# A recurrent attention and two experts on one core: weights to floats in fewer VectorE steps, and TensorE tied to the written order

## The chip, the cores and the metric

The kernel runs on one core of a Trainium2 chip. The metric is the time of one execution on the device in microseconds (us), the median of several runs. The kernel before takes 1247.12 us (three runs, 1245.66 to 1247.34). A core has TensorE (PE in the profile; its weight loads are PEld), VectorE (DVE), ScalarE (ACT), GpSimd (POOL) and SyncE (SP, which issues most of the DMAs here).

## What is computed

Three stages follow each other. The sizes are batch 4, 8 heads, 768 steps of time, head size 40; 3072 tokens of width 320; 2048 and 1536 columns in the two experts.

```
# 1. attention: a 40x40 state per batch and head, updated at each of 768 steps
y[t]  = r[t] @ state
Sa    = state @ a[t]
state = state * w[t] - outer(Sa, b[t]) + outer(v[t], k[t])
# 2. first expert
h = x @ w_in;  g = max(h, 0) + alpha * min(h, 0);  x = g @ w_out
# 3. second expert
g = x @ w_gate;  out = (silu(g) * (x @ w_val)) @ w_out
```

The weights of the experts arrive as 64-bit floats, since the reference multiplies by a 64-bit scalar when it draws them. The kernel reads them as pairs of 32-bit words and makes 32-bit floats of them itself.

## The kernel before, in words

**Blocks and items.** Time is cut into six blocks of 128 steps (m = 0 to 5), each with four items, one for each batch row. An item holds all eight heads and is worked in two chunks of 64 steps (`L`).

**Preparing an item** (`prep_a`, `prep_b`, seven steps). Scans on VectorE make running products of the decays w (L502, L509), a product of these with a gives the tile `AN` (L519, two halves of 64 partitions; the other halves are zeroed by GpSimd, L517), one with b and k gives `kbt` (L531). Then TensorE forms 16 products `mnp` (L543) and 8 transposes `kbp` (L571), which ScalarE and GpSimd bring to SBUF. The raw inputs w and a lie in one tile `raw_wa`, loaded by two DMAs an item.

**The inverse** (`inverse`, forty steps, once a block). When four items are prepared, their 64 by 64 triangular matrices are inverted: 31 small steps on VectorE, each a product and a subtraction (L604, L612), between transposes (L589 ahead, L615 and L617 behind), and then small matmuls on TensorE (L625, L644). Its work tiles share their buffers (tag "kbt") with `kbt` of the preparation from block one on, so that the next block's preparation starts behind the inverse.

**Running an item** (`seq`, thirteen steps). The state goes from chunk to chunk: a chunk transposes the state into `sp` (L707, copied to `s0` by ScalarE, L709), and then forms `zp` (L714), `pp` (L724, with transposes L730), `gp` (L741) and `yp` (L756, L760), one after the other in one PSUM buffer of its chain, with copies by ScalarE and VectorE between. Two chains of items run side by side. The result goes to DRAM (`xd`).

**The first expert on a block** (`mlp1`). For each of 16 slices of 128 columns ("groups" below): eight matmuls of 512 columns up (L238), ReLU on ScalarE (L277), the leaky part on VectorE (L278), a split into a high and a low part (L184, L185), and eight matmuls down (L243 to L249). A block is 36 steps: a load of x, two steps a group, and three that bring out the result.

**Weights.** `conv` loads 128 rows or columns of a weight, `narrow` makes floats, `split` cuts them, and they go back to DRAM (`wd`), from where `fetch` takes them for each block. `narrow` is three VectorE steps on the two words (L172 to L174), an absolute value on ScalarE (L175), and a comparison that sets tiny values to zero: on VectorE (L177) for the 32 pieces of the first expert, on GpSimd (L179, L180) for others. The first expert's pieces are converted beside blocks zero and one (`conv1`), those of the second partly beside the last blocks (`conv2`, 12 pieces), partly in the tail (`direct`, 24 pieces).

**What sets the order.** The program is written by `drive`, which takes steps from several generators in turn, so that each is about equally far along; each generator's weight is its number of steps. A planner then places the instructions of every engine by priority (`tc.cur_priority`, lower is earlier) and by simulated times. Preparing, inverting and running items have priorities 3000 ahead (`SQ`, `PRI`), so that matmuls of the first expert fill in behind. In turn m of the main loop stand together: running block m, preparing and inverting block m+1, and the first expert on block m-1, all 36 steps of it; in the last turn 15 of them are held back for the tail, where the first expert on block five follows.

**The second expert** runs at the end alone, six blocks of 12 slices.

Of the kernel before, what the change touches and what calls it, by code (L numbers as in the profile page):

```python
# [9 lines left out]
U32 = mybir.dt.uint32  # L10
ACTF = mybir.ActivationFunctionType
# [4 lines left out]
FAC = 1.0  # L16
# [48 lines left out]
LOOK = 2  # L65
KEEP = 4

@with_exitstack
def kernel(
# [50 lines left out]
    def drive(*gens, lead=0, engs=0, lag=1, who=0):  # L120
        live = [[*g, 0, j] for j, g in enumerate(gens)]
        names = ["PE", "DVE", "Activation", "Pool"]
        while live:
            e = min(live, key=lambda e: e[3] / e[1])
            try:
                tc.cur_priority -= e[2]
                with ExitStack() as st:
# [6 lines left out]
                    ok = next(e[0], 0)  # L134
                    if e[4] < lead:
# [6 lines left out]
                e[3] += 1  # L142
# [21 lines left out]
    LEAST = 1.125 * 2.0 ** -15  # L164

    def narrow(pool, raw, dve=0):
        whi, wlo = raw[..., 1], raw[..., 0]
# [19 lines left out]
    def conv(stage, idx, src, f, kind, into=None, dve=None):  # L187
# [10 lines left out]
        w32 = narrow(stage, raw, idx < 2 * K1 if dve is None else dve)  # L198
# [196 lines left out]
    for j, pool in ((0, rawp), (1, bp)):  # L395
        for nm in ("wa", "bk"):
            t = raw[nm, j] = pool.tile([128, 2, NP, TB], F32, name=f"raw_{nm}{j}")
            for n in range(2):
                for q in (1, 3):
                    eng = nc.vector if nm == "wa" and j == 0 else nc.gpsimd  # L400
                    eng.memset(t[32 * q:32 * q + 32, n], 1.0 if (nm, n) == ("wa", 0) else 0.0)
# [43 lines left out]
    def load(i, nm):  # L445
# [3 lines left out]
        t = raw[nm, rset(i)]  # L449
        for h, pr in enumerate(halves):  # L450
            nc.sync.dma_start(out=t[pr], in_={"wa": wa, "bk": bk}[nm][m, bb, h])
# [40 lines left out]
    def prep_a(i):  # L492
        m, bb = order[i]
        it = items[i] = {}
        rw = raw["wa", rset(i)][:, 0]
# [18 lines left out]
        ra = raw["wa", rset(i)][:, 1]  # L514
# [71 lines left out]
    def inverse(m):  # L586
# [8 lines left out]
        for kk in range(HALF - 1):  # L595
# [17 lines left out]
            yield  # L613
# [41 lines left out]
    N_PREP, N_INV, N_SEQ, N_MLP = 7, 40, 13, 2 * K1 + 4  # L655
# [5 lines left out]
    def seq(i, ch, own=None):  # L661
# [33 lines left out]
        for c in range(CPB):  # L695
# [9 lines left out]
            sp = ps_s.tile([128, NP // 2, 128], F32, tag=sb, name="sp")  # L705
            for q in range(NP // 2):
                nc.tensor.transpose(sp[:, q, :], st[:, 2 * q:2 * q + 2, :].rearrange("q p d -> q (p d)"), ident)  # L707
            s0 = seq_p.tile([128, NP // 2, 128], F32, tag="s0", name="s0")
            nc.scalar.copy(out=s0, in_=sp)  # L709
            yield  # L710
# [16 lines left out]
            for h in range(2):  # L727
                nc.scalar.mul(out=pv[:, h::2, c, h], in_=pp[:, 0, h::2], mul=-1.0)
# [302 lines left out]
```

## Time and profile before

| | |
|---|---|
| median of three runs | 1247.12 us |
| span of the profiled execution | 1243.4 us |
| PE busy, PEld busy | 1095.8 us (88%), 928.7 us (75%) |
| DVE, ACT, POOL busy | 781.3, 592.6, 312.6 us |
| the chain that ended last, by engine | PE 52%, DVE 20%, ACT 10%, DMA 8%, issue 6% |

The span is the time from the first to the last instruction of the execution that was profiled; its own time is the span and what lies around it, and the runs' median is 3.7 us above the span. A row of the window view gives the busy time of each engine in a stretch, in brackets its instructions, then TensorE's granted clock (1.00 is 2.4 GHz, 0.50 is 1.2 GHz), the DMA engines' share and GB/s. A row of the line view gives busy time and the mean ns of one instruction, and behind the second bar the idle time of the engine just ahead of them with what ended it.

### The profile page before, as it was taken

Reading aid. Unit: us, or ns where it says so; the run is one execution under the profiler, and the core shown is the slowest. Engines: PE = TensorE matmul, PEld = TensorE weight load, DVE = VectorE, ACT = ScalarE, POOL = GpSimd, SP = SyncE. Lnnn points to the kernel's source line nnn. Section 1 sums busy time; section 2 is a strip of 40 time slices with the busy share of each in tenths; the row PEclk is TensorE's granted clock in tenths of the full one; section 3 lists DMA queues with packets and bytes.
Section 4 is the critical chain, followed back from the end, with each engine's and each line's share of the span. In section 5 each row is a group of like instructions: output and inputs, shape, how many; then the busy total and the mean of one; then the engine's idle time right before and its main releaser. Section 6 shows DMA issues by size and latency. Waiting matters only on the chain.

```text
span 1243.4 us, 24467 instructions
## 1 busy us (share of the span) xinstructions
PE 1095.8 (88%) x9056; PEld 928.7 (75%) x9056; DVE 781.3 (63%) x1689; ACT 592.6 (48%) x1463; POOL 312.6 (25%) x502
## 2 busy tenths in 40 slices
PE   3345787899799989989999899999999999999998
PEld 2244577777687777777777687888888888888887
DVE  7999999898669758974967444677732323232222
ACT  4547448844763674477455533455432323232222
POOL 9425443613121222252126300334500000000000
PEclk9658697999899999999999999999999999999999
DMA  5534577874545454464448648865210101000000
GB/s 149 168 115 133 180 257 251 263 228 126 161 127 176 134 161 142 144 196 145 145 139 266 201 131 292 283 213 153 73 47 1 47 1 38 1 22 1 22 1 22
DMA packets 92486, 166.36 MB, mean 134 GB/s; under 512 B 12752, under 2 KB 42704, under 8 KB 92368
## 3 DMA queue, kind: packets, MB, share of 16 engines
q1 hardware_dynamic: 84208, 160.87, 41.2%
q10 hardware_dynamic: 8160, 3.93, 1.1%
q8 instruction: 72, 1.18, 0.4%
q14 instruction: 46, 0.38, 0.1%
HBM read 136.98 MB, written 27.79 MB: 133 GB/s over the span
## 4 chain that ended last, share of the span: by engine, by line
PE 52%; DVE 20%; ACT 10%; DMA 8%; issue 6%; POOL 3%; SPq 1%; ACTq 0%; DVEq 0%; POOLq 0%
PE pg L238 10%; PE pv L238 10%; PE u L238 8%; PE o L952 3%; PE o L951 3%; PE o L953 3%; DVE la L612 3%; DVE tmp L604 3%; DMA raw_wa<-in_wa_dram 2%; PE gp L741 2%; PE d L243 2%; DMA xa<-xd 2%; PE d L244 2%; PE d L245 2%; DVE gs L685 2%
## 5 line engine op out<-in xcount | busy, mean ns | idle before, releaser
L184 ACT CAST gh<-g 128x512 fp32r<-128x512 f32 (+1 forms) x176 | 105.9, 602 | 175.2 <-DVE g L967 116.7
L967 DVE TENSOR_TENSOR g<-pv,sg 128x512 f32<-128x512 f32 x72 | 49.8, 691 | 200.1 <-PE pv L238 200.0
L185 DVE TENSOR_TENSOR gl<-g,gh 128x512 fp32r<-128x512 f32 (+1 forms) x176 | 119.5, 679 | 77.0 <-ACT gh L184 76.2
L238 PE MATMUL u<-xh,wt 128*128 128x512 f32 (+1 forms) x416 | 147.6, 397 | 15.9 <-DVE g L278 12.6
L278 DVE SCALAR_TENSOR_TENSOR g<-g,neg,u 128x512 f32<-128x512 f32 (+1 forms) x104 | 72.9, 701 | 63.0 <-ACT g L277 62.4
L238 PEld LDWEIGHTS u<-xh,wt 128*128 128x128 f32 x416 | 79.0, 193 | 34.9 <-DVE g L278 16.8
L238 PE MATMUL pg<-xh,w 128*128 128x512 f32 x288 | 102.0, 394 | 0.7 <-ACT sg L965 0.7
L965 ACT ACTIVATE sg<-pg 128x512 f32<-128x512 f32 x72 | 43.0, 597 | 124.3 <-PE pg L238 124.3
L238 PE MATMUL pv<-xh,w 128*128 128x512 f32 x288 | 100.5, 389 | 0.0
L277 ACT ACTIVATE g<-u 128x512 f32<-128x512 f32 (+1 forms) x104 | 58.7, 564 | 81.6 <-PE u L238 65.0
L543 PE MATMUL mnp<-AN,kbt 128*128 128x128 f32 x384 | 60.7, 311 | 32.1 <-POOL la L591 15.9
L952 PE MATMUL o<-w,gh 128*128 128x320 f32 x288 | 87.7, 309 | 0.0
L951 PE MATMUL o<-w,gh 128*128 128x320 f32 x288 | 87.1, 308 | 0.0
L244 PE MATMUL d<-gl,wt 128*128 128x512 f32 (+1 forms) x208 | 80.9, 391 | 1.2 <-DVE gl L185 1.2
L699 POOL COPY gs<-raw_v 64x160 f32<-64x160 f32 x96 | 42.3, 441 | 157.7 <-PE yp L756 70.1
L543 PEld LDWEIGHTS mnp<-AN,kbt 128*128 128x128 f32 x384 | 54.3, 219 | 36.2 <-POOL AN L517 17.6
L604 DVE TENSOR_TENSOR tmp<-la 128x96 f32<-128x96 f32 (+43 forms) x306 | 78.6, 281 | 3.2 <-POOL la L592 1.3
L238 PE MATMUL u<-xl,wt 128*128 128x512 f32 (+1 forms) x208 | 80.2, 386 | 0.2 <-DVE xl L185 0.2
L612 DVE TENSOR_TENSOR la<-la,tmp 128x96 f32<-128x96 f32 (+43 forms) x306 | 77.6, 278 | 1.9
L245 PE MATMUL d<-gh,wt 128*128 128x512 f32 (+1 forms) x208 | 78.5, 380 | 0.0
L557 POOL TENSOR_SCALAR_AFFINE_SELECT AN<-AN 64x256 f32<-64x256 f32 x96 | 48.5, 505 | 117.9 <-ACT AN L556 88.8
L953 PE MATMUL o<-w,gl 128*128 128x320 f32 x288 | 76.1, 309 | 0.0
(118 smaller groups left out, 2678.6 us busy)
## 6 DMA issues: line engine op xcount, KB each, us to landing
wt<-wd SPq DMA_DIRECT2D x98, 384.0 KB
wt<-wd SPq DMA_DIRECT2D x98, 320.0 KB
wd<-wc SPq DMA_DIRECT2D x24, 384.0 KB
raw<-in_moe_w_out_dram SPq DMA_DIRECT2D x28, 320.0 KB
raw_wa<-in_wa_dram SPq DMA_DIRECT2D x48, 160.0 KB
raw_bk<-in_bk_dram SPq DMA_DIRECT2D x48, 160.0 KB
wd<-wc SPq DMA_DIRECT2D x20, 320.0 KB
raw<-in_moe_w_in_dram SPq DMA_DIRECT2D x16, 256.0 KB
```

The lines of the kernel that those rows point to most:

```text
L184: nc.scalar.copy(out=h, in_=raw)
L185: eng.tensor_tensor(out=l, in0=raw, in1=h.bitcast(F32), op=ALU.subtract)
L238: nc.tensor.matmul(ps, lt, rh, start=(i == 0), stop=(i == len(ops) - 1))
L244: nc.tensor.matmul(ps, wh, gl, start=False, stop=False)
L245: nc.tensor.matmul(ps, wl, gh, start=False, stop=last)
L278: nc.vector.scalar_tensor_tensor(g, g, neg[:, f:f + 1], ps, ALU.mult, ALU.add)
L543: nc.tensor.matmul(ps[:, s].rearrange("p h t -> p (h t)"), kbt[:, g * SH + s].rearrange("p j t -> p (j t)"), an[:, :, g * SH + s, :],)
L604: nc.vector.tensor_tensor(out=tv, in0=ml[:, kk + 1:HALF, kk:kk + 1].to_broadcast([128, nr, ns]), in1=tl[:, kk:kk + 1, c0:c0 + ns].to_broad ...
L612: mark["inv"] = nc.vector.tensor_tensor(out=dst, in0=dst, in1=tv, op=ALU.subtract)
L951: nc.tensor.matmul(ops[q], gh[:, ts], wh, start=first, stop=False)
L952: nc.tensor.matmul(ops[q], gh[:, ts], wl, start=False, stop=False)
L953: nc.tensor.matmul(ops[q], gl[:, ts], wh, start=False, stop=last)
```

## The change

Weights: `narrow` lets ScalarE scale the high word by 2^-112 and make a float's three last bits of the low word's upper 16 bits, and then takes two VectorE steps; the comparison is gone, on either engine. Preparation: w and a get tiles of their own; a lies in a tile whose cross halves are zero from the start, and `AN` is one VectorE instruction over 128 partitions and 1024 elements. An item's w and a are loaded by four DMAs of half the size. Running: the transposes of the state move behind `pp`, into its PSUM buffer, and their copy behind that of the U part; the stage of its own for `sp` goes. Order: from turn two on (`TIE`), each TensorE instruction depends on the one written ahead of it, and the priorities there are zero; the second chain starts half a step later; a step of the inverse counts 0.6 of a step; the first expert runs 6 of its steps later (`LAG`), which is three slices of two steps, and 19 steps are left for the tail, 4 more than before.

```diff
-        nc.vector.tensor_scalar(y, whi, 0x07FFFFFF, 3, ALU.bitwise_and, ALU.logical_shift_left)
-        nc.vector.scalar_tensor_tensor(z, whi, 0xC0000000, y, ALU.bitwise_and, ALU.bitwise_or)
-        nc.vector.scalar_tensor_tensor(y, wlo, 29, z, ALU.logical_shift_right, ALU.bitwise_or)
-        nc.scalar.activation(out=f, in_=whi.bitcast(F32), func=ACTF.Abs)
-        if dve:
-            nc.vector.scalar_tensor_tensor(f, f, LEAST, y.bitcast(F32), ALU.is_ge, ALU.mult)
-            return f
-        nc.gpsimd.tensor_scalar(f, f, LEAST, None, ALU.is_ge)
-        nc.gpsimd.tensor_tensor(out=f, in0=f, in1=y.bitcast(F32), op=ALU.mult)
+        nc.scalar.activation(out=f, in_=whi.bitcast(F32), func=ACTF.Copy, scale=2.0 ** -112)
+        nc.scalar.activation(out=y, in_=wlo, func=ACTF.Copy, scale=2.0 ** -13, bias=2.0 ** -14 - 0.5)
+        nc.vector.scalar_tensor_tensor(y, whi, 0x80000000, y, ALU.bitwise_and, ALU.bitwise_or)
+        nc.vector.scalar_tensor_tensor(z, z, 3, y, ALU.logical_shift_left, ALU.bitwise_or)
...
+    def tied(new):
+        for x in new:
+            if x.engine == nc.tensor.engine:
+                if tail_pe:
+                    tc.add_manual_dep(
+                        x, tail_pe.pop().name,
+                        mybir.DependencyInfo(mybir.DependencyClass.NoSync, mybir.DependencyReason.DATA),
+                        reason="order of TensorE",
+                    )
+                tail_pe.append(x)
...
-            nc.sync.dma_start(out=t[pr], in_={"wa": wa, "bk": bk}[nm][m, bb, h])
+            if nm == "wa":
+                nc.sync.dma_start(out=raw["w", rset(i)][pr, 0], in_=wa[m, bb, h][:, 0])
+                nc.sync.dma_start(out=raw["a", rset(i)][pr, h], in_=wa[m, bb, h][:, 1])
...
-        for h, pr in ((0, hi), (1, lo)):
-            nc.gpsimd.memset(an[pr, h], 0.0)
-        for h, pr in ((0, lo), (1, hi)):
-            (nc.gpsimd if i >= B and ANP >> h & 1 else nc.vector).tensor_tensor(
-                out=an[pr, h], in0=ra[pr].rearrange(seg, c=CPB), in1=wx[pr, ::-1, 0:L], op=ALU.mult
-            )
+        nc.vector.tensor_tensor(
+            out=an, in0=raw["a", rset(i)].rearrange("q h p (c t) -> q h (p c) t", c=CPB),
+            in1=wx[:, ::-1, 0:L].unsqueeze(1).to_broadcast([128, 2, NSEG, L]), op=ALU.mult,
+        )
...
-    N_PREP, N_INV, N_SEQ, N_MLP = 7, 40, 13, 2 * K1 + 4
+    N_PREP, N_INV, N_SEQ, N_MLP = 7, 9 + (HALF - 1) * INVW, 13, 2 * K1 + 4
...
-            sp = ps_s.tile([128, NP // 2, 128], F32, tag=sb, name="sp")
...
+            sp = pp[:, 0].rearrange("p (a b) t -> p a (b t)", b=2)
...
+    gm = chain(*gms)
+    held = 2 * (K1 - HOLD) + 3 + HELD
     for m in range(1, NM):
         s0_ = m * B
+        sp_, hp_ = (0, 0) if m >= TIE else (SQ, HP)
...
-        gm = gms[m - 1]
-        nm = N_MLP + (1 if FA and m == 1 else 0)
-        held = 2 * (K1 - HOLD) + 3 if m + 1 == NM else 0
-        g.append((take(gm, nm - held), nm, 0))
...
-        drive(*g, lead=2, engs=G2, lag=LG2, who=W2)
...
+        nm = N_MLP - (LAG if m == 1 else held - LAG if m + 1 == NM else 0)
+        g.append((take(gm, nm), nm, 0))
+        drive(*g, tie=m >= TIE)
```

## Rows read from the trace of the kernel before

**Rows 1.** The windows view: stretches between ends of inverses, and what follows.
```profile
78.00:190.00 112.00, 81.30 (x994) 70.57 (x996) 106.29 (x267) 67.01 (x196) 48.84 (x76) 0.78 0.57 182
190.00:300.00 110.00, 97.36 (x1070) 84.67 (x1067) 99.05 (x239) 71.11 (x204) 39.54 (x65) 0.91 0.72 227
...
411.00:522.00 111.00, 101.16 (x1113) 83.07 (x1112) 83.00 (x207) 65.77 (x178) 25.43 (x53) 1.00 0.51 151
...
632.00:750.00 118.00, 109.12 (x1138) 87.69 (x1137) 64.98 (x113) 58.64 (x144) 41.12 (x53) 0.99 0.59 185
750.00:854.00 104.00, 101.67 (x432) 81.56 (x430) 66.51 (x106) 50.32 (x90) 29.17 (x27) 0.98 0.73 247
```

**Rows 2.** The chain of waits around 300 us (start, us, what).
```profile
299.56 2.00 DVE tt L617
```

**Rows 3.** The windows view of line L172 alone: pieces of weights converted.
```profile
78.00:190.00 112.00, 6.81 (x17) 0.78 0.57 182
190.00:300.00 110.00, 4.12 (x9) 0.91 0.72 227
```

**Rows 4.** The chain of waits in the tail: matmuls of 512 columns.
```profile
1227.11 1.81 PE pv L238 x8
```

**Rows 5.** The timeline of PE: runs of one kind (start, us, what).
```profile
411.88 1.15 PE L724 MATMUL pp<-tt,zs 128*64 128x64 f32 x32
412.96 2.21 PE L625 MATMUL eps<-la,tt 32*32 32x32 f32 x128
415.11 0.50 PE L243 MATMUL d<-gh,wt 128*128 128x512 f32 x1
...
564.52 1.95 PE L741 MATMUL gp<-rbd,pv 128*128 128x128 f32 x16
566.30 0.27 PE L571 MATMUL kbp<-ident,kbt 128*128 128x128 f32 x1
...
569.72 0.93 PE L756 MATMUL yp<-gs,KB 128*64 128x104 f32 x16
570.49 0.61 PE L760 MATMUL yp<-rbd,s 128*64 128x128 f32 x8
570.92 0.88 PE L756 MATMUL yp<-gs,KB 128*64 128x104 f32 x16
```

**Rows 6.** The windows view of line L278 alone: groups of the first expert.
```profile
411.00:522.00 111.00, 9.64 (x13) 1.00 0.51 151
...
632.00:750.00 118.00, 12.63 (x17) 0.99 0.59 185
750.00:854.00 104.00, 18.62 (x25) 0.98 0.73 247
```

**Rows 7.** The line view: the inverse's steps, `narrow`, `AN` and `kbt`.
```profile
L604 DVE TENSOR_TENSOR tmp<-la 128x96 f32<-128x96 f32 (+43 forms) x306 | 78.6, 281 | 3.2 <-POOL la L592 1.3
...
L612 DVE TENSOR_TENSOR la<-la,tmp 128x96 f32<-128x96 f32 (+43 forms) x306 | 77.6, 278 | 1.9
...
L173 DVE SCALAR_TENSOR_TENSOR wz<-raw,wy 128x384 uint32<-128x384 uint32 (+1 forms) x68 | 47.6, 700 | 3.6 <-POOL w L185 1.7
...
L174 DVE SCALAR_TENSOR_TENSOR wy<-raw,wz 128x384 uint32<-128x384 uint32 (+1 forms) x68 | 45.0, 661 | 0.9
...
L175 ACT ACTIVATE wz<-raw 128x384 f32<-128x384 f32 (+1 forms) x68 | 36.1, 531 | 63.4 <-DVE wy L174 37.7 <-issue 8.8 <-POOL la L592 4.1
...
L519 DVE TENSOR_TENSOR AN<-raw_wa,Wx 64x512 f32<-64x512 f32 x48 | 35.4, 737 | 1.1
...
L531 DVE TENSOR_TENSOR kbt<-raw_bk,rest 128x1024 f32<-128x1024 f32 x24 | 30.5, 1269 | 7.8 <-PE kbp L571 6.8 <-PE eps L625 0.8
...
L172 DVE TENSOR_SCALAR wy<-raw 128x384 uint32<-128x384 uint32 (+1 forms) x68 | 27.1, 399 | 21.7 <-POOL wz L180 17.1 <-DMA raw<-in_moe_w_val_dram 2.2 <-DMA raw<-in_moe_w_out_dram 1.1
...
L177 DVE SCALAR_TENSOR_TENSOR wz<-wz,wy 128x384 f32<-128x384 f32 (+1 forms) x44 | 23.8, 542 | 10.1 <-ACT wz L175 9.8
```

**Rows 8.** The view of waits: us in total, times, longest us.
```profile
PEld zp L714 <- ACT s L709: 18.8, 13, 5.0
```

More of the change, by code (lines that the diff above doesn't have):

```diff
@@ L10 @@
 U32 = mybir.dt.uint32
+U16 = mybir.dt.uint16
 ACTF = mybir.ActivationFunctionType
@@ L65 @@
 LOOK = 2
+LAG = 6
+HELD = 4
+INVW = 0.6
+TIE = 2
 KEEP = 4
@@ L118, in traced, with drive @@
         return nc.cur_bb.bb.instructions
-    def drive(*gens, lead=0, engs=0, lag=1, who=0):
-        live = [[*g, 0, j] for j, g in enumerate(gens)]
+    tail_pe = []
+    def tied(new):
[8 more added lines that the diff above has]
+                tail_pe.append(x)
+    def drive(*gens, lead=0, engs=0, lag=1, who=0, tie=False):
+        live = [[*g[:3], g[3] if len(g) > 3 else 0, j] for j, g in enumerate(gens)]
         names = ["PE", "DVE", "Activation", "Pool"]
@@ L134, in drive @@
                     ok = next(e[0], 0)
+                    if tie:
+                        tied(traced()[n0:])
                     if e[4] < lead:
@@ L185, in split, with conv @@
         eng.tensor_tensor(out=l, in0=raw, in1=h.bitcast(F32), op=ALU.subtract)
-    def conv(stage, idx, src, f, kind, into=None, dve=None):
+    def conv(stage, idx, src, f, kind, into=None):
         sw = words(src)
@@ L395 @@
     for j, pool in ((0, rawp), (1, bp)):
-        for nm in ("wa", "bk"):
-            t = raw[nm, j] = pool.tile([128, 2, NP, TB], F32, name=f"raw_{nm}{j}")
-            for n in range(2):
+        for nm in ("w", "bk"):
+            sh = [128, 2, NP, TB] if nm == "bk" else [128, 1, NP, TB]
+            t = raw[nm, j] = pool.tile(sh, F32, name=f"raw_{nm}{j}")
+            for n in range(sh[1]):
                 for q in (1, 3):
-                    eng = nc.vector if nm == "wa" and j == 0 else nc.gpsimd
-                    eng.memset(t[32 * q:32 * q + 32, n], 1.0 if (nm, n) == ("wa", 0) else 0.0)
+                    eng = nc.vector if nm == "w" and j == 0 else nc.gpsimd
+                    eng.memset(t[32 * q:32 * q + 32, n], 1.0 if nm == "w" else 0.0)
+        t = raw["a", j] = pool.tile([128, 2, NP, TB], F32, name=f"raw_a{j}")
+        (nc.vector if j == 0 else nc.gpsimd).memset(t, 0.0)
         if j == 0:
@@ L732, in seq @@
                 )
+            for q in range(NP // 2):
+                nc.tensor.transpose(sp[:, q, :], st[:, 2 * q:2 * q + 2, :].rearrange("q p d -> q (p d)"), ident)
             for h, pr in ((0, lo), (1, hi)):
@@ L737, in seq @@
                 )
+            s0 = seq_p.tile([128, NP // 2, 128], F32, tag="s0", name="s0")
+            nc.scalar.copy(out=s0, in_=sp)
             yield
@@ L870 @@
         )
+    gm = chain(*gms)
+    held = 2 * (K1 - HOLD) + 3 + HELD
     for m in range(1, NM):
         s0_ = m * B
+        sp_, hp_ = (0, 0) if m >= TIE else (SQ, HP)
         g = [
-            (chain(seq(s0_, 0), seq(s0_ + 2, 0)), 2 * N_SEQ, SQ),
-            (chain(seq(s0_ + 1, 1), seq(s0_ + 3, 1)), 2 * N_SEQ, SQ),
+            (chain(seq(s0_, 0), seq(s0_ + 2, 0)), 2 * N_SEQ, sp_),
+            (chain(seq(s0_ + 1, 1), seq(s0_ + 3, 1)), 2 * N_SEQ, sp_, .5),
         ]
         if m + 1 < NM:
-            g.append((chain(preps(range((m + 1) * B, (m + 2) * B)), lift(inverse(m + 1), PV)), FAC * (B * N_PREP + N_INV), HP))
-        gm = gms[m - 1]
-        nm = N_MLP + (1 if FA and m == 1 else 0)
-        held = 2 * (K1 - HOLD) + 3 if m + 1 == NM else 0
-        g.append((take(gm, nm - held), nm, 0))
-        if not CG:
-            g.append((take(c2, CS[m - 1]), CS[m - 1], 0))
-        drive(*g, lead=2, engs=G2, lag=LG2, who=W2)
-        if CG:
-            for _ in take(after(mark["inv"], c2), CS[m - 1]):
-                pass
-        assert held or next(gm, 0) == 0
+            g.append((chain(preps(range((m + 1) * B, (m + 2) * B)), lift(inverse(m + 1), PV)), FAC * (B * N_PREP + N_INV), hp_))
+        nm = N_MLP - (LAG if m == 1 else held - LAG if m + 1 == NM else 0)
+        g.append((take(gm, nm), nm, 0))
+        drive(*g, tie=m >= TIE)
+        for _ in take(after(mark["inv"], c2), CS[m - 1]):
+            pass
     ap_.close()
```

32 lines of the change are left out of this document (14 added, 18 removed).

## The prediction

> **What bounds the kernel now.** I read the windows first [rows 1], cut where an inverse ends (L617; the one at 299.56 us stands in [rows 2]), then the lines, then runs of matmuls in the timeline. They show three regimes. Up to 300 us VectorE is the full engine: 106.29 of 112 us and 99.05 of 110 us, while TensorE has 81.30 and 97.36 at a granted clock of 0.78 and 0.91, between its two levels of 1.2 and 2.4 GHz [rows 1]. In this stretch the first expert's 32 pieces of weights are made floats; 17 and 9 of them fall into these two windows, the other 6 ahead [rows 3]. From 300 to 750 us neither engine is full by itself: in 411 to 522 us VectorE has 83.00 of 111 us, ScalarE 65.77, TensorE 101.16 by its spans [rows 1]. These spans overlap and include stalls, so I count TensorE's work at the pace of clean runs. From 750 us on one stream of matmuls follows another and little is to be won.
>
> The paces: 512 columns take 1.81/8 = 0.227 us [rows 4]; 128 columns on the full array (566.30 - 564.52)/16 = 0.111; `yp` 0.77/16 = 0.048 and its second part 0.43/8 = 0.054; `pp` 1.08/32 = 0.034; the inverse's small ones 2.15/128 = 0.017 [rows 5]. A group of the first expert is 16 matmuls of 512 columns, 3.63 us. Attention of one block, counts from the code: 64 `mnp`, 32 `kbp`, 64 `gp`, 32 transposes of state and U at 0.111 make 21.3 us; 128 `yp` 6.2, 64 of its second part 3.5, 128 `pp` 4.3, 128 `zp` at the pace of `pp` 4.3, 256 of the inverse 4.3: 43.9 us. The window 411 to 522 us holds 13 groups [rows 6], 47.2 us; with 43.9 that is 91.1 of 111 us, a share of 0.82. The last, 632 to 750 us, holds 17 groups (61.7 us) and attention without preparation and inverse (96 matmuls and 256 fewer: 43.9 - 10.7 - 4.3 = 28.9 us), 90.6 of 118 us, 0.77. Three blocks of 91.1 and this one make 364 of 450 us: 0.81.
>
> The Trainium skill ("Perfetto Trace Analysis", section "Identifying the Most-Contended Engine") says that the busy time of matmuls misjudges TensorE's headroom, and that the busy share of weight loads is the measure. By matmul spans 10 us of the 111 would be idle, by weight loads (83.07) 28 us; the count above gives 20, between them. By the matmul spans, about 10 us in each of four blocks would be all that an order could win.
>
> **The change part by part.**
>
> *Floats, first expert.* A piece loses four VectorE steps, 0.399 + 0.700 + 0.661 + 0.542 = 2.30 us, and gets two of the two-operand kind. No row shows their exact operations; the nearest are L173 and L174, mean 0.68, so 1.36 us, and 0.94 us are saved [rows 7]. Between 78 and 300 us that is 26 x 0.94 = 24.4 us. The 6 pieces ahead stand beside loads and the first inverse; I count 2 us of their 5.6. ScalarE gets one activation more, about 0.53 us [rows 7], 13.8 us in a stretch where it has 138 of 222 us [rows 1]: its room covers it. If it had none, those 13.8 us would come off the gain. If VectorE runs these steps only where it would else be idle, the gain is nothing; if the two new steps ran at the 0.54 of L177, it would be 1.22 x 32 = 39 us.
>
> *AN.* Twice 0.737 becomes one instruction of the shape of `kbt`, 1.269 us [rows 7]: 0.2 us saved an item, 1.6 us for the 8 items of blocks one and two, in the same full engine. Two GpSimd memsets an item go too; GpSimd is at 49 of 112 us, so I cost this at nothing. Four loads for two: 48 DMA issues more on SP in all. The w tile is free after its copy already, the a tile only after `AN`; an a load that waits holds the second w load and whatever is behind in SP's queue, as the combined load did. I cost it at nothing, and between -3 and +3 us.
>
> Together the stretch to 300 us shortens by 24.4 + 2 + 1.6 = 28 us, to 272, bounds 0 to 40. What is late next there is the inverse's own chain, and TensorE, whose clock can only gain from denser work.
>
> *Order, lag and held steps.* These say what each turn must hold. Turn one gets 30 of the first expert's steps, turns two to four 36 each, which is 16 groups, and turn five 36 - (19 - 6) = 23, of which 6 finish block three's expert (1.5 groups and three steps of result), one loads x and 16 are 8 groups: 9.5 groups. So TensorE's work is 3 x (58.0 + 43.9) = 305.7 us and 34.5 + 28.9 = 63.4 us, together 369 us between 272 us and the end of attention. Before, 13 groups fitted in a turn and the backlog was worked off in the last; with the order tied, a turn cannot end ahead of its 16 groups.
>
> At what share will TensorE run? Not below the present 0.81 if the waits are the same ones; not above 1. What speaks for more: `zp` no longer stands behind the copy of the state, for which the weight loads alone waited 18.8 us [rows 8]; expert matmuls come in whole steps between those of attention, where before they filled in behind; and x is loaded 6 steps into a turn, not right behind its store. The nearest row for a stream whose order is that of the program, with the same activations on ScalarE and VectorE between, is 750 to 854 us: 25 groups, 90.7 of 104 us, 0.87 [rows 1, 6]. I take 0.87: 369/0.87 = 424 us, where 0.81 gives 455 and 1 gives 369. A turn is then 101.9/0.87 = 117 us, longer than today's 111, and the last 73 where it was 118.
>
> *Moved transposes.* Their count stays (32 a block with those of U). They now wait for the two negated copies of `pp`, and `gp`, written after them, is held in TensorE's queue; `gp` needs these copies anyway. In the share above; alone between -5 and +2 us a block.
>
> *Second expert's floats.* 12 pieces beside the last blocks and 24 in the tail lose a VectorE step or two and two of GpSimd. TensorE is at 101.67 of 104 us there [rows 1]; nothing.
>
> *The tail.* From 750 us to the end of the span it took 493.4 us with 25 groups [rows 6]; 19 steps held are 8 groups and the result, with 16 of block five 24 groups: 493.4 - 3.6 = 490 us.
>
> The sum: 272 + 424 + 490 = 1186 us against the profiled span of 1243.4; with the 3.7 us by which the median of the runs shown stands over this span, 1190.
>
> **The rivals.**
>
> *The order gives nothing.* The share stays 0.81, since the waits are for ScalarE and VectorE, whose work the order does not shorten: 455 instead of 424 us, 1221. For it: VectorE has 83 of 111 us already and would have 3 groups more in a turn.
>
> *The first stretch doesn't shorten.* Conversion has the lowest priority there, and the chain of scans, inverse and chunks may set the pace. Then only some 5 us come off, and the time is 1190 + 23 = 1213. Against: VectorE has 6 us idle in 112.
>
> *Stalls of the strict order: slower.* The place is the inverse. Its 31 steps now count 18.6 of 28 + 27.6 = 55.6, a third of a turn, 39 us of 117. In it VectorE owes a sixth of 156 us of L604 and L612 [rows 7], 26 us, and a third of the rest of its turn: (83 + 3 x 1.4 - 26) / 3 = 20. That is 46 us in 39, some 7 over; if what is late there (a group's low part, the inverse's last step) then holds TensorE, everything written behind it waits, though it is ready. At 7 us a turn the share of 0.87 becomes 0.83, and the time 1211. It is slower than before only from a share of 369/(1247 - 3.7 - 272 - 490) = 0.766 down, which is 19 us a turn more than I count; at 0.75 it is 1258. For it: VectorE is the engine with the least room in this third. Against: its steps can slide into the final sixth, where it has few. The Trainium skill ("TensorE: Matmul & The Clock Gate", step-by-step section of Part 2) says that matmuls stay in program order and only weight loads are pulled ahead; by that rule a late operand stops the whole stream, in either kernel; the trace agrees as far as the stop of `zp`'s loads shows it [rows 8].
>
> *More than forecast.* A share of 0.95 and 33 us in the first stretch: 267 + 388 + 490 + 3.7 = 1149. For it: runs of one kind follow each other without a gap [rows 4, 5]. Against: no stretch of mixed work as long as a turn comes near it.
>
> **How the numbers follow.** My forecast, shares of 0.84 to 0.91 and 20 to 33 us ahead, has 0.5 and its own range is 1166 to 1213. The order without effect has 0.18, the first stretch unshortened 0.12, both at once, which is 1244 and no change, 0.02, stalls that make it slower 0.08, and more than forecast 0.10. The range is 1150 to 1226: it reaches the second and third case and leaves out the stalls and half of the last. Faster by over 0.2%, which is about what a measurement of this kernel can tell from no change, has 0.90, within 0.2% 0.02, slower 0.08.
>
> **What would show it.** VectorE's two steps a piece at 0.6 to 0.7 us, and inverses ending near 272, 389, 506 and 623 us. 16 calls of the leaky step in each of these three turns, where 13 stood. The last chunk of attention ends near 696 us, and 490 us follow, 24 groups and the second expert. If the first inverse in this row ends at 272 but the next 125 us or more later, the order is what failed; if it ends beyond 290, the conversion was no load on the path. A busy VectorE with TensorE waiting for it in the last half of each turn would show the stalls, and an end of attention beyond 753 us would refute the forecast's sign.

## The result, and the profile after

The changed kernel takes 1261.84 us (median of four, 1255.15 to 1265.51) where the kernel before took 1247.23 beside it: 1.0113 times as long, interval 1.0077 to 1.0149. I had forecast 1190 with a range of 1150 to 1226 and given slower 0.08. The profiled span is 1257.9 us against 1243.4, 14.5 us more.

The windows view of the changed kernel, cut at the ends of the inverses and of attention as in [rows 1]; the columns are the same:

```profile
78.00:186.00 108.00, 81.02 (x1002) 71.78 (x997) 101.21 (x232) 79.78 (x232) 49.77 (x77) 0.80 0.70 223
186.00:296.00 110.00, 96.93 (x1104) 85.05 (x1101) 85.02 (x216) 68.29 (x197) 29.35 (x57) 0.91 0.65 202
296.00:403.00 107.00, 97.14 (x1045) 78.16 (x1043) 79.54 (x195) 65.23 (x173) 20.13 (x40) 1.00 0.51 152
403.00:530.00 127.00, 115.72 (x1164) 93.99 (x1166) 86.80 (x209) 70.11 (x184) 22.19 (x48) 0.96 0.50 145
530.00:649.00 119.00, 111.69 (x1134) 90.38 (x1128) 80.69 (x201) 69.57 (x182) 24.26 (x49) 0.96 0.50 153
649.00:756.00 107.00, 94.74 (x1072) 77.32 (x1070) 51.10 (x94) 58.19 (x147) 21.01 (x35) 0.95 0.56 177
756.00:863.00 107.00, 104.43 (x450) 83.75 (x448) 61.80 (x91) 57.02 (x110) 15.88 (x16) 1.00 0.74 252
```

The end of inverse two in its chain of waits, the place of [rows 2]:

```profile
296.30 1.91 DVE tt L633
```

Its windows view of line L192 alone (the first VectorE step of a piece, as [rows 3]), and behind the dots of L291 alone (groups of the first expert, as [rows 6]):

```profile
78.00:186.00 108.00, 14.10 (x20) 0.80 0.70 223
186.00:296.00 110.00, 4.79 (x6) 0.91 0.65 202
...
296.00:403.00 107.00, 10.34 (x14) 1.00 0.51 152
403.00:530.00 127.00, 11.86 (x16) 0.96 0.50 145
530.00:649.00 119.00, 11.15 (x15) 0.96 0.50 153
649.00:756.00 107.00, 9.71 (x13) 0.95 0.56 177
756.00:863.00 107.00, 18.61 (x25) 1.00 0.74 252
```

Its line view, for the lines of [rows 7] and for the first ScalarE step of a piece (L190):

```profile
L620 DVE TENSOR_TENSOR tmp<-la 128x96 f32<-128x96 f32 (+43 forms) x306 | 79.6, 285 | 1.9
...
L192 DVE SCALAR_TENSOR_TENSOR wy<-raw,wy 128x384 uint32<-128x384 uint32 (+1 forms) x68 | 52.0, 764 | 31.9 <-ACT wy L191 29.6 <-DMA wt<-wd 1.6
...
L193 DVE SCALAR_TENSOR_TENSOR wz<-wz,wy 128x384 uint32<-128x384 uint32 (+1 forms) x68 | 36.6, 538 | 2.5
L190 ACT ACTIVATE wz<-raw 128x384 f32<-128x384 f32 (+1 forms) x68 | 36.0, 530 | 46.3 <-DMA raw<-in_moe_w_gate_dram 12.5 <-DMA raw<-in_moe_w_in_dram 11.0 <-DMA raw<-in_moe_w_val_dram 10.0
...
L534 DVE TENSOR_TENSOR AN<-raw_a,Wx 128x1024 f32<-128x1024 f32 x24 | 32.4, 1352 | 3.5 <-DMA raw_a<-in_wa_dram 3.1
```

Read against [rows 1, 3]: the work did what it says. A piece costs VectorE 0.764 + 0.538 = 1.30 us (I had taken 1.36). VectorE's busy time up to inverse two falls from 106.29 + 99.05 to 101.21 + 85.02 us, 19 us. But inverse two is done at 298 us instead of 302 (by the cuts of the windows at 296 instead of 300, where I had forecast 272); beyond 290, I had written, conversion was no load on the path. Attention ends at 756 us, beyond the 753 that were to refute the sign. The second window shows it best: VectorE now stands idle for 25 of 110 us, and the window is as long as before. From inverse two to the end of attention 460 us go by, where there were 450 (300 to 750); the last groups of the first expert take 107 us for 104; the rest of the tail 394.9 for 389.4. By these cuts that is the account of the 14.5 us: -4, +10, +3 and +5.5.

In the middle the waits changed their kind more than their sum. The view of waits of TensorE from 300 us to the end of attention, first the kernel before (300 to 750 us):

```profile
PE kbp L571 <- ACT AN L556: 8.8, 4, 7.2
PE u L238 <- DVE g L278: 6.6, 9, 1.0
```

and the changed kernel (296 to 756 us):

```profile
PE u L251 <- DVE g L291: 18.4, 11, 3.5
PE eps L641 <- DVE la L631: 6.1, 2, 3.1
```

All rows of these two answers sum to 36.0 and 40.2 us. The tied order spares `kbp` its waits and lets `u` and the inverse's matmuls wait for VectorE in their stead. The granted clock in the four turns was 0.95, 1.00, 0.98, 0.99 before and is 1.00, 0.96, 0.96, 0.95 now; between its two levels of 1.2 and 2.4 GHz. Taken on TensorE's busy time in these windows, what is missing to 1.00 makes 8 and 14 us, an estimate, 6 us more. So about 4 us of the middle's 10 are waits and about 6, by this estimate, the clock. More work it is hardly: the view of L291 has 58 groups there for 56, but of the expert's matmuls themselves 915 stand there for 906, which is 2 us.

In the tail one wait explains 4 us, and the timeline of the changed kernel shows how it comes about (start, us, what; in brackets the idle time ahead and what ended it):

```profile
861.68 0.55 ACT L190 ACTIVATE wz<-raw 128x384 f32<-128x384 f32 x1 [3.19 <-DMA raw<-in_moe_w_val_dram]
...
864.66 1.28 ACT L979 ACT_TABLE_LOAD   x1
865.96 0.60 ACT L979 ACTIVATE sg<-pg 128x512 f32<-128x512 f32 x1
...
866.61 0.80 PE L251 MATMUL pg<-xh,w 128*128 128x512 f32 x1 [4.63 <-ACT sg L979]
```

The first step of a conversion is ScalarE's now. It stands 3.19 us for its transfer, the rest of the conversion, copies of the first expert's result and a table load of 1.28 us follow, the `silu` behind them comes late, and TensorE stands 4.63 us. In the kernel before its wait for the same `silu` is 0.7 us.

### The profile page after: what moved, and what is told of

It reads as the page before. It is cut to its first block, busy times and chain, and to the rows that moved or that the text cites. A ratio compares the mean times of both kernels' runs of the same rounds, so it can differ in the third digit from the quotient of the medians.

```text
span 1257.9 us, 24374 instructions
## 1 busy us (share of the span) xinstructions
PE 1106.5 (88%) x9056; PEld 936.7 (74%) x9056; DVE 729.8 (58%) x1552; ACT 621.5 (49%) x1531; POOL 231.5 (18%) x405
## 4 chain that ended last, share of the span: by engine, by line
PE 56%; DVE 17%; ACT 11%; DMA 10%; issue 4%; SPq 1%; POOL 0%; ACTq 0%; DVEq 0%; POOLq 0%
PE pg L251 10%; PE pv L251 10%; PE u L251 9%; PE o L966 3%; PE o L965 3%; PE o L967 3%; DVE tmp L620 3%; DVE la L628 3%; DMA xd<-pv 2%; PE gp L757 2%; DMA raw<-in_moe_w_in_dram 2%; PE d L256 2%; PE d L257 2%; PE d L258 2%; PE mnp L559 2%
## 5 line engine op out<-in xcount | busy, mean ns | idle before, releaser
L251 PE MATMUL u<-xh,wt 128*128 128x512 f32 (+1 forms) x416 | 153.6, 411 | 24.4 <-DVE g L291 21.4
L198 DVE TENSOR_TENSOR gl<-g,gh 128x512 fp32r<-128x512 f32 (+1 forms) x176 | 118.3, 673 | 87.9 <-ACT gh L197 85.6
L291 DVE SCALAR_TENSOR_TENSOR g<-g,neg,u 128x512 f32<-128x512 f32 (+1 forms) x104 | 72.9, 701 | 86.8 <-ACT g L290 86.2
L251 PEld LDWEIGHTS u<-xh,wt 128*128 128x128 f32 x416 | 81.6, 199 | 47.2 <-DVE g L291 26.6
L256 PE MATMUL d<-gh,wt 128*128 128x512 f32 (+1 forms) x208 | 79.4, 412 | 6.3 <-ACT gh L197 3.3
L573 POOL TENSOR_SCALAR_AFFINE_SELECT AN<-AN 64x256 f32<-64x256 f32 x96 | 51.1, 533 | 163.9 <-ACT AN L572 145.1
L258 PE MATMUL d<-gh,wt 128*128 128x512 f32 (+1 forms) x208 | 79.4, 383 | 0.0
```

Of the source, the lines that this page charges most:

```text
L198: eng.tensor_tensor(out=l, in0=raw, in1=h.bitcast(F32), op=ALU.subtract)
L251: nc.tensor.matmul(ps, lt, rh, start=(i == 0), stop=(i == len(ops) - 1))
L256: nc.tensor.matmul(ps, wh, gh, start=first, stop=False)
L258: nc.tensor.matmul(ps, wl, gh, start=False, stop=last)
```

## The experiments

*Parts of the change.* First the new `narrow` in the kernel before, for all weights (e1), and the changed kernel with TensorE's order free in all turns, which by the same constant also puts the priorities 3000 ahead in all of them (e2). The ratio behind each time is to the kernel before, run beside it; the changed kernel's is 1.0113. Two runs on different chips compare best by these ratios.

```diff
 e1, from before
+        nc.scalar.activation(out=f, in_=whi.bitcast(F32), func=ACTF.Copy, scale=2.0 ** -112)
+        nc.scalar.activation(out=y, in_=wlo, func=ACTF.Copy, scale=2.0 ** -13, bias=2.0 ** -14 - 0.5)
+        nc.vector.scalar_tensor_tensor(y, whi, 0x80000000, y, ALU.bitwise_and, ALU.bitwise_or)
+        nc.vector.scalar_tensor_tensor(z, z, 3, y, ALU.logical_shift_left, ALU.bitwise_or)
 e2, from after
-TIE = 2
+TIE = 99
```

> The kernel before with the new conversion of weights alone. Theory A (the loop of preparation, inverse and next preparation sets the pace, and conversion only fills VectorE's gaps around it): the inverse of block two ends at 292 to 300 us as in both kernels, and the time is 1240 to 1250 us. Rival B (the floats do shorten the first stretch, and the new order gave it back): that inverse ends near 275 us and the time is 1215 to 1228 us.

> The changed kernel with the order of TensorE left free in all turns and the priorities 3000 ahead in all of them; lag, held steps and weights of the steps stay. Theory A (the tied order puts groups of the expert ahead of the next block's preparation, whose stretches took 75 us in turns three and four instead of 57 and 63): these stretches go back to 55 to 63 us, and the time is 1225 to 1242 us. Rival C (lag, held steps and step weights lose, not the tie): stretches of 70 us or more stay, and the time is 1252 us or more.

e1: 1271.21 us, 1.0174 (1.0121 to 1.0226). e2: 1273.32 us, 1.0182 (1.0129 to 1.0235). e1 is slower than either theory had it, and its inverse two ends at 296 us, where theory A put it. e2's time is rival C's, while its inverses do come closer (395, 507, 602 us where the changed kernel has 403, 530, 649), as theory A said. The ends of the inverses are not what sets the end. The order without the tie is no better: 11 us slower, 9 by the ratios, which e9 and e10 will show to be within what a new plan moves.

Then the weight of preparation and inverse in the written order (e3, e4):

```diff
 e3, from after
-            g.append((chain(preps(range((m + 1) * B, (m + 2) * B)), lift(inverse(m + 1), PV)), FAC * (B * N_PREP + N_INV), hp_))
+            g.append((chain(preps(range((m + 1) * B, (m + 2) * B)), lift(inverse(m + 1), PV)), (0.7 if m >= TIE else FAC) * (B * N_PREP + N_INV), hp_))
 e4, from after
-INVW = 0.6
+INVW = 1.0
```

> The changed kernel, still tied from turn two on, but there the preparation and the inverse are written at a weight of 0.7 of their steps, so ahead of the expert's groups. Theory A: the stretch of preparation falls from 75 to about 60 us, the inverses of blocks three to five come some 112 us apart, and the time is 1235 to 1248 us. Rival D (waiting in strict order costs by itself, wherever the steps are written): turns stay near 120 us and the time is 1255 us or more.

> The changed kernel with an inverse's step counted as 1 instead of 0.6. Theory A: preparation is then written in the first 41% of a turn instead of 50%, its stretch falls by some 10 us, the inverse's grows by some 4, and the time is 1242 to 1255 us. Rival D: within 0.4% of the changed kernel, 1257 to 1267 us.

e3: 1257.54 us, 1.0062 (1.0031 to 1.0092). e4: 1266.14 us, 1.013 (1.0082 to 1.0178). Both times are rival D's. Where the inverse is written moves the time by 4 us either way (-6 and +2 by the ratios), which the intervals do not tell from nothing.

Then the floats by halves, old ones for the second expert in the changed kernel (e5), new ones in the kernel before for the first (e6) or the second expert alone (e7), and e5 with e3's edit (e8):

```diff
 e5 and e8, from after
+        w32 = narrow(stage, raw) if idx < 2 * K1 else narrow_old(stage, raw, dve)
 e6, from before
+        w32 = narrow_new(stage, raw) if idx < 2 * K1 else narrow(stage, raw, dve or 0)
 e7, from before
+        w32 = narrow(stage, raw, 1) if idx < 2 * K1 else narrow_new(stage, raw)
```

> The changed kernel, but the second expert's 36 pieces are converted as before (three VectorE steps and ScalarE's absolute value, the comparison on GpSimd or VectorE); the first expert's 32 stay new. Theory F (the new first step sits on ScalarE and waits there for the raw weights' DMA, some 15 us in the tail where the kernel before had none; the first expert's ReLU and split stand behind it in ScalarE's queue): some 10 to 15 us come off, 1246 to 1252 us. Rival G (the new conversion costs nothing there, the loss is the order's): 1257 to 1266 us.

> The kernel before with the new conversion for the first expert's 32 pieces alone. Theory F: no loss in the tail; the first stretch gains little, as TensorE's lost time up to 300 us was the same in all kernels so far (150 to 153 us): 1240 to 1250 us. Rival G2 (the new conversion disturbs the first two blocks' plan): 1260 us or more.

> The kernel before with the new conversion for the second expert's 36 pieces alone. Theory F: it carries the loss of the run with both, 1260 to 1272 us, with ScalarE waiting 10 us or more for raw weights behind 760 us. Rival G2: 1243 to 1252 us.

> The changed kernel with the second expert's pieces converted as before and preparation and inverse written at 0.7 of their weight. Theory F with theory A: both gains add, 1236 to 1246 us, at or below the kernel before. Rival G: 1253 us or more, as the run with the weight alone.

e5: 1258.23 us, 1.0079 (1.0053 to 1.0106), and its view of waits lists none of TensorE behind 860 us. That is rival G's time, though the wait of `silu` is real: in the profiled run all behind the end of attention takes 495.0 us (from 758.5) instead of 501.9, and attention ends 2.5 us later. At 4 us the whole is worth less than a new plan moves. e6: 1264.74 us, 1.0111 (1.0064 to 1.0157). e7: 1267.33 us, 1.0155 (1.0112 to 1.0197). e8: 1258.22 us, 1.0079 (1.0048 to 1.011). e6's time is rival G2's, e7's theory F's; in e8 the two gains don't add, as rival G has it. Nor do the parts: by their ratios e6 and e7 would make 33 us together, and e1, which is both, made 22, a difference barely outside the intervals. That pointed at the planner.

*The same work planned anew.* Four kernels change no instruction's work, only the order that the planner finds:

```diff
 e9, from before
-SQ = 3000
+SQ = 2990
 e10, from before
-PRI = 3000
+PRI = 2990
 e11, from before, and e12, from after (the products of zp alone)
-                for h, pr in ((0, lo), (1, hi)):
+                for h, pr in ((1, hi), (0, lo)):
```

> The kernel before with the priority of running items 2990 ahead instead of 3000: no instruction more or less, no size changed, but the planner lays out another order (652 lines of TensorE's order differ). Theory H (the order of the kernel before is one that fits unusually well, and any new plan of the same work loses 10 to 20 us, so the parts tried alone measured the new plan and not their own work): 1255 us or more. Rival I (a new plan of the same work comes out within 4 us, so the parts' losses are their own): 1243 to 1251 us.

> The kernel before with the priority of preparation and first inverse 2990 ahead instead of 3000, nothing else: 724 lines of TensorE's order differ. Theory H: 1255 us or more. Rival I: 1243 to 1251 us.

> The kernel before with the two halves of each pair of zp products written the other way round: the same matmuls, 755 lines of TensorE's order differ. Theory H: 1255 us or more. Rival I: 1243 to 1251 us.

> The changed kernel with the same swap of the two halves of zp: 146 lines of TensorE's order differ, as the tie holds most of it. Theory H: it stays near the changed kernel, 1252 to 1268 us, as that plan is an ordinary one. Rival I: within 0.4% of it too, so this run tells how far a new plan moves a tied kernel.

e9: 1260.99 us, 1.0112 (1.0084 to 1.014). e10: 1259.54 us, 1.0093 (1.0068 to 1.0119). e11: 1250.1 us, 1.0027 (1.0003 to 1.0051). e12: 1258.35 us, 1.0081 (1.0053 to 1.0109), 3.5 us under the changed kernel. A priority of 2990 for 3000 costs nearly as much as the whole change. All three new plans of the kernel before are slower than its own, two of them as theory H has it; e11 lies in rival I's range. So its plan seems to be one that fits well, and an edit may give it up, which three plans suggest and don't prove. Gains and losses of a part below some 14 us can't be told from this.

*Is VectorE's conversion on the path?* In e13 the two VectorE steps are left out for the first expert's 32 pieces (the floats of its weights are unfinished then), in e14 the first of them is done three times, which changes no result:

```diff
 e13, from after (times is 0 for the first expert, else 1)
+        for _ in range(times):
+            nc.vector.scalar_tensor_tensor(y, whi, 0x80000000, y, ALU.bitwise_and, ALU.bitwise_or)
+            nc.vector.scalar_tensor_tensor(z, z, 3, y, ALU.logical_shift_left, ALU.bitwise_or)
 e14, from after (times is 3 for the first expert, else 1)
+        for _ in range(times):
+            nc.vector.scalar_tensor_tensor(y, whi, 0x80000000, y, ALU.bitwise_and, ALU.bitwise_or)
```

> The changed kernel with the two VectorE steps of narrow left out for the first expert's 32 pieces (the floats of its weights are wrong; the two ScalarE scalings stay): 32 x 1.30 = 42 us of VectorE less, 34 us of it before 300 us. The same work merely planned anew has moved the time by 0 to 13 us, so less than that tells nothing. Theory J (conversion only fills gaps of VectorE; the loop preparation, inverse, next preparation sets the pace and the first expert follows it): 1248 to 1270, the second inverse ends within 6 us of 296. Rival K (VectorE's queue in the first 300 us is on the path): second inverse ends by 275, time at or under 1240.

> The changed kernel with the first VectorE step of narrow done three times for the first expert's 32 pieces (doing it again changes nothing in the result): 64 x 0.764 = 49 us of VectorE more, 40 us of it before 300 us. Theory J: 1255 to 1275, second inverse within 8 us of 296. Rival K: second inverse ends at 320 or later, time at or over 1285.

e13: 1251.05 us, 1.0042 (1.0017 to 1.0068). e14: 1274.15 us, 1.0229 (1.0204 to 1.0254). The line view of e13, both VectorE steps, and then of e14, the first:

```profile
L193 DVE SCALAR_TENSOR_TENSOR wy<-raw,wy 128x384 uint32<-128x384 uint32 (+1 forms) x36 | 30.3, 841 | 26.1 <-ACT wy L191 24.9 <-DMA raw<-in_moe_w_val_dram 0.7
...
L194 DVE SCALAR_TENSOR_TENSOR wz<-wz,wy 128x384 uint32<-128x384 uint32 (+1 forms) x36 | 19.5, 542 | 1.9
```

```profile
L193 DVE SCALAR_TENSOR_TENSOR wy<-raw,wy 128x384 uint32<-128x384 uint32 (+1 forms) x132 | 85.7, 649 | 35.2 <-ACT wy L191 33.2 <-DMA raw<-in_moe_w_val_dram 1.0
```

The end of inverse two in the timeline of e13, then e14:

```profile
283.63 1.87 DVE L634 STREAM_TRANSPOSE tt<-la 128x1024 f32<-128x1024 f32 x1
```

```profile
316.98 1.87 DVE L634 STREAM_TRANSPOSE tt<-la 128x1024 f32<-128x1024 f32 x1
```

And the windows view of e13 up to there:

```profile
78.00:175.00 97.00, 64.74 (x744) 57.19 (x744) 69.41 (x172) 73.37 (x213) 46.97 (x69) 0.71 0.67 219
175.00:284.00 109.00, 99.31 (x1228) 88.25 (x1222) 81.31 (x220) 65.31 (x193) 25.68 (x56) 0.97 0.59 183
```

Neither theory holds: J has both times in its ranges and neither end of inverse two, K none of the four. In e13 VectorE has (52.0 - 30.3) + (36.6 - 19.5) = 38.8 us less, inverse two ends 13 us earlier, and 11 us come off the time (9 by the ratios). In e14 its first step has 33.7 us more, inverse two ends 21 us later, and the time is 12 us longer (14 by the ratios). Some quarter to two fifths of VectorE's time arrives at the end, about a third. Each of the two differences is no larger than what a new plan has cost; for the work, and not the plan, speaks only that they have opposite signs. And without any such step the stretch still lasts until 285.5 us, with VectorE idle for 28 of 97 and 28 of 109 us.

*What sets a turn?* e15 leaves out every second step of the inverse for blocks one to five, e16 products of the low parts of x and g in the first expert (4 of a group's 16 matmuls; the last rows of x and g, which are stacked, keep theirs), e17 does both, and e18 is e16's edit in the kernel before:

```diff
 e15 and e17, from after
-        for kk in range(HALF - 1):
+        for kk in range(0, HALF - 1, 2 if m else 1):
 e16 and e17, from after, and e18, from before (up, for the first expert; down)
-            ops += [(t[:, j], xh[:, j]), (t[:, j], xl[:, j]), (t[:, 3 + j], xh[:, j])]
+            ops += [(t[:, j], xh[:, j]), (t[:, 3 + j], xh[:, j])]
...
-            nc.tensor.matmul(ps, wh, gl, start=False, stop=False)
```

> The changed kernel with every second of the inverse's 31 steps left out for blocks one to five (the inverses are wrong): about 13 us of VectorE less in each turn, 66 us in all. If the loop preparation, inverse, next preparation sets the pace (theory J), the ends of the inverses come about 13 us closer to each other, that of block five by 590 rather than 649, and the time falls to 1200 to 1225, the rest lost where TensorE's expert work is left over at the end of attention. If TensorE's own work sets the pace (rival T), the inverses end earlier but the last piece of the first expert's x does not, and the time stays in 1245 to 1270.

> The changed kernel without the products of the low parts of x and g in the first expert (its result is less exact): 4 of each group's matmuls of 512 columns left out, at 0.22 us each 0.89 us a group, 79 groups up to 756 us and 25 behind: 70 us and 22 us of TensorE less. VectorE, ScalarE and the DMAs keep their work. Rival T (TensorE's own work sets the pace up to the end of attention): near 1262 - 92 = 1170, in 1160 to 1190. Theory J (the loop of preparation and inverse sets it): the 22 us behind attention come off and little of the 70, 1225 to 1245.

> The changed kernel with both: every second step of the inverse left out for blocks one to five, and the products of the low parts of x and g left out in the first expert (e15 gave 0 and e16 gave 27 us of the 92 left out, 22 of them behind attention). Theory B (in the written order of TensorE the chain through VectorE and TensorE's own work run out at nearly the same moment, so that either alone hides what the other gains): together clearly more than 27 us, turns of about 110 us rather than 122, 1195 to 1218. Theory J2 (neither is on the path, another chain such as the items' recurrence or the hand-over of x through DRAM sets the turn): 1228 to 1240, the turns as in e16.

> The kernel before with the products of the low parts of x and g left out in the first expert: the same 92 us of TensorE less as in e16, but with TensorE's order free for the planner in all blocks. If TensorE's work set the pace of the kernel before, as the prediction had it (share of TensorE as the rate of the middle): 1247 - 92 = 1155, in 1150 to 1180. If its chains are as near as in the changed kernel: 1210 to 1230. Re-planning alone moves it by 0 to 13 us.

e15: 1261.42 us, 1.0118 (1.0097 to 1.0139). e16: 1234.85 us, 0.9911 (0.9892 to 0.9929). e17: 1205.23 us, 0.967 (0.9655 to 0.9686). e18: 1219.78 us, 0.9784 (0.9758 to 0.981).

The 92 us of the expectations count all 104 calls as whole groups; 16 of them are half ones, and the matmuls left out make 87 us, 24 of them behind attention. Against the changed kernel's 1261.84, half the inverse is worth 0, the 87 us of matmuls 27, and both together 57 (-1, 25 and 55 by the ratios). e15 came out as rival T has it and e16 as theory J: each says that the other's work sets the pace. The end of one inverse and the start of the next in the timelines show how the one hides the other. The changed kernel:

```profile
352.53 2.03 DVE L605 STREAM_TRANSPOSE la<-tt 128x1024 f32<-128x1024 f32 x1 [0.26 <-ACT tt L568]
...
403.34 1.91 DVE L633 STREAM_TRANSPOSE tt<-la 128x1024 f32<-128x1024 f32 x1
...
478.24 2.02 DVE L605 STREAM_TRANSPOSE la<-tt 128x1024 f32<-128x1024 f32 x1 [0.26 <-ACT tt L568]
...
606.06 2.02 DVE L605 STREAM_TRANSPOSE la<-tt 128x1024 f32<-128x1024 f32 x1 [0.26 <-ACT tt L568]
```

e15, with the end of inverse two ahead: the inverse of block three is done 24 us earlier, and the next one starts only 2 us earlier. The likely reason, not tested by itself, is that its preparation has its place in TensorE's order: the first `mnp` come at 433.8 us there and at 437.8 in the changed kernel.

```profile
257.14 1.95 DVE L633 STREAM_TRANSPOSE tt<-la 128x1024 f32<-128x1024 f32 x1
...
379.13 1.87 DVE L633 STREAM_TRANSPOSE tt<-la 128x1024 f32<-128x1024 f32 x1
...
475.96 2.02 DVE L605 STREAM_TRANSPOSE la<-tt 128x1024 f32<-128x1024 f32 x1 [0.26 <-ACT tt L568]
```

e16, where the products left out bring that start 8 us ahead, and e17 with 26 us:

```profile
470.57 2.02 DVE L604 STREAM_TRANSPOSE la<-tt 128x1024 f32<-128x1024 f32 x1 [0.73 <-ACT tt L567]
```

```profile
336.78 2.00 DVE L604 STREAM_TRANSPOSE la<-tt 128x1024 f32<-128x1024 f32 x1 [0.73 <-ACT tt L567]
...
452.33 2.00 DVE L604 STREAM_TRANSPOSE la<-tt 128x1024 f32<-128x1024 f32 x1 [0.72 <-ACT tt L567]
...
575.59 2.01 DVE L604 STREAM_TRANSPOSE la<-tt 128x1024 f32<-128x1024 f32 x1 [0.73 <-ACT tt L567]
```

What TensorE is spared in e16 it waits instead, as the view of its waits from 300 to 756 us says (all rows 66.5 us, the changed kernel 40.2):

```profile
PE u L251 <- DVE g L290: 19.5, 9, 5.6
PE eps L640 <- DVE la L630: 19.5, 3, 7.9
```

Behind attention, too, only 6 us of the 24 come off in e16.

e17's time is that of its theory B (in e1 and e2 the letter stood for another): the chain through VectorE and TensorE's own stream hold the time together, so that the first alone brings nothing, the second alone a third of its 87 us, and both twice that, which is more than a new plan has moved. Its turns, 116 and 123 us from start to start of an inverse for 126 and 128, are shorter, but not the 110 of the theory. With some 150 us of work taken away 57 came off, so a third limit stands close behind; the items' recurrence and the hand-over of x, which theory J2 named, were not taken away in any run. e18 is 27 us faster than before as well: with the planner free, as small a share of the 87 us arrives. Whether the inverse hides the rest there was not tried.

## Why the prediction was wrong

**What held.** The paces and most counts: 1.30 us a piece on VectorE for 1.36; 14, 16 and 15 groups in the three turns up to the last inverse where I had 16 in each; 25 groups behind attention where I had 24. AN was off by a little: 1.352 us for the 1.269 of `kbt`'s shape, so 0.12 us saved an item instead of 0.2.

**The first stretch: 28 us forecast, 3 to 4 measured.** This step failed first. I took VectorE for the bound of the stretch, since it was busy for 205 of 222 us, and moved its saved time to the end one for one. The sentence "what is late next there is the inverse's own chain, and TensorE" had no number. The runs give it. In e13, even with none of the first expert's VectorE steps, inverse two ends at 285.5 us, 16 us ahead of before, so sparing steps of conversion alone did not reach 272. In e15, with all of the conversion in place and half the steps of inverses one and two, it ends at 259 us, 39 us ahead of the changed kernel: the inverse's own chain was late next. And of these 39 us nothing arrives at the end, as 15 groups of the expert stand ahead of that point for 21 (calls of L291), and TensorE has the others still to do. So the second half of the step, that the end of the stretch moves the end of the kernel one for one, failed as well. TensorE's clock, which was to gain, stayed at 0.80 and 0.91 for 0.78 and 0.91. By the rate of e13 and e14, about a third of VectorE's time, 28 us would be some 9. That only 3 came may partly be conversion itself, which fills in where VectorE is free: 20 pieces went into the first window where 17 had been [rows 3]. The rest of the difference is within what new plans of the same work move.

**The share of TensorE: 0.87 forecast, 0.80 measured (369 of 460 us).** This is the larger failure, 36 us. I took 0.87 from the stretch behind attention, whose stream has no inverse, no preparation and no recurrence beside it. It asked for 36 of the 40 us of waits that the changed kernel shows in this stretch to go. What the tied order removes are some waits, and others take their place; what bounds the whole are at least two things at once. e15, e16 and e17 show it: 0, 27 and 57 us.

The three turns up to the last inverse took 107, 127 and 119 us, together the 353 that I had forecast (3 x 117 = 351), with 45 groups for 48. The 34 us are missing in the last stretch, 107 us for 73, with 13 groups for 9.5: a share of 0.71 by my count, where I had used 0.87 throughout and [rows 1, 6] had shown 0.77 for the same stretch before. No preparation runs there and of the inverse only its closing matmuls, and in e17 it is no shorter, 108 us (602.7 to 711.1). What holds it was not isolated.

The Trainium skill ("Perfetto Trace Analysis", section "Identifying the Most-Contended Engine") would read TensorE's headroom from its weight loads, beside a count of its arithmetic. They are busy for 340 of these 460 us; no order tried here (e2, e3, e4, e12) turned any of this quarter into time beyond the noise.

The rival "the order gives nothing" described what came of this step. Its reason, that the waits are for engines whose work the order doesn't shorten, fits the waits listed, 40 us; they are less than half of the 89 us by which the stretch exceeds my count of 371 for its 58 groups, and the clock makes some 14 more by the estimate above.

**The tail: 490 us forecast, 502 measured.** By the calls of the leaky step it is one group more than forecast; by the expert's matmuls themselves, 416 behind 756 us where 400 stood behind 750, it is two, 7 us. The wait of `silu` is 4.6, and e5, which takes it away, has 7 us less behind attention. That is the 12. I cost the second expert's floats at nothing because TensorE was full; but the edit put a wait for a DMA at the head of a step on ScalarE, and behind it stood work that TensorE needs.

**The rivals' chances.** I gave "the order gives nothing" 0.18, "the first stretch doesn't shorten" 0.12 and both at once 0.02, as if they were independent. The runs suggest one cause: a kernel whose engines run out together gives little for one of them. Both at once is what came, and its price of 1244 lacks what the tail and the middle added. The stalls of the strict order that I feared at the inverse exist (6.1 us of `eps` and 18.4 of `u`), but they replace other waits: the sum is 4 us more, and an untied order (e2) is no better.

**Left open.** Which of the 14 us belong to the change and which to the luck of a plan can't be told: new plans of unchanged work cost 3 to 14 us in the kernel before. What else bounds the first stretch in e13, with VectorE idle for a quarter of it, was not tried, nor what holds the last stretch of attention. One other plan of the changed kernel's unchanged work was tried (e12, 1258 us), so whether some plan of it reaches 1247 is open. No version faster than the kernel before that does all its work was found.

## What to carry to other kernels

Before crediting an engine's saved time, price what is late next: take the time away in an ablation, and take it away from the second candidate too, because 0 and 27 us alone can be 57 together. An earlier end of one stretch is no gain by itself: look whether work was left over for the next, as in e15. Where a planner orders the work, first run a neutral edit to learn how far the plan alone moves the time; here it was 3 to 14 us, as much as the change. When a step moves to another engine, look at what its first instruction waits for, and what then stands behind it in that engine's queue.

## What the runs showed of the hardware that was not expected

Two VectorE instructions of the same kind and shape, 128x384 (some 128x320) with two operands, differ by two fifths in the mean: 0.764 us for L192, 0.538 for L193. One operand of L192 is every second word of the raw tile, but that is not it: e14 does L192 twice more on the same operands, and these passes take (85.7 - 52.0) / 64 = 0.53 us, if its first passes cost what they did. The timelines show what goes with it. Of the 68 passes of L192 in the changed kernel, the 28 with no GpSimd instruction beside them take 0.58 us at most, 0.53 in the mean. The 40 that overlap one take 0.93 in the mean. The 27 longest, 0.87 to 1.66 us, all stand beside GpSimd's subtraction L198 and end 0.33 to 0.42 us after it does, as here (start, us, what; VectorE's timeline, then GpSimd's):

```profile
784.99 0.56 DVE L192 SCALAR_TENSOR_TENSOR wy<-raw,wy 128x384 uint32<-128x384 uint32 x1
...
787.92 1.08 DVE L192 SCALAR_TENSOR_TENSOR wy<-raw,wy 128x384 uint32<-128x384 uint32 x1
...
787.57 1.02 POOL L198 TENSOR_TENSOR w<-wz,w 128x384 fp32r<-128x384 f32 x1 [44.72 <-ACT w L197]
```

So the longer time looks like a wait for GpSimd inside the instruction's span, and VectorE's busy time contains it. L193, which overlaps L198 only twice in its 68 passes, hardly has it. A run with L198 on another engine was not made.

The granted clock was lower where TensorE's work had been taken away. A turn of e16 in its windows view:

```profile
397.00:519.00 122.00, 103.64 (x1088) 84.38 (x1088) 86.06 (x209) 69.67 (x184) 21.58 (x48) 0.92 0.50 151
```

The turn of the changed kernel from 403 us on has 0.96. On 103.64 us of busy time the difference is 4 us, an estimate, and so a part of what the products left out did not bring.
